# Retention and two expert layers on one core: moved refills, gathers, weight splits and row turns around the expert stage

## The chip, the cores and the metric

The kernel runs on one core of one Trainium2 chip. The metric is the device time of that core in microseconds (us), the median of several executions. TensorE (PE) multiplies matrices, its weight loads are shown apart as PEld, VectorE is DVE, ScalarE is ACT, GpSimd is POOL, and SyncE (SP) issues most of the plain transfers. POOL issues the gathers and scatters that go by a list of row numbers.

## The reference

```python
# stage 1: retention, per head a decayed state (q, k, v: 2 x 8 x 768 x 64)
state = gamma * state + k[t] v[t]^T ;  y[t] = scale * q[t] state
x = y as 1536 tokens x 512
# stage 2: a dense layer, 512 -> 2048 -> 512
h = x @ w_in ;  g = maximum(0.01 * h, h) ;  x = g @ w_out
# stage 3: 8 experts, each token goes to one of them; an expert takes at most capacity = 384 tokens
logits = x @ w_gate ;  e = argmax(logits) ;  gate = softmax(logits)[e]
for each expert: h = maximum(rows @ w1[e], 0) ;  y = h @ w2[e]        # 512 -> 1024 -> 512
out[token] = gate * y                                                # zero for tokens over capacity
```

## The kernel before, in words

All of it is one program, whose order on each engine is the order in which the code is written. The matrices are multiplied in split form: a value is a high part `hi` (made by ACT) and a low part `lo` (made by DVE), and three products are summed.

The dense layer works on units of 128 of the 2048 hidden columns for blocks of 384 tokens (`unit_h`, `unit_y`; lines 363 and 414 are its matmuls). Behind a block's last unit its rows go to `x2d` in HBM (`store_rows`), and `route` finds the expert of each token: logits, the one-hot `oh` (line 495), positions by a matmul (line 505).

Once three quarters of the tokens are routed, one expert is chosen ahead (`choose`). Its weights are gathered by POOL into `praw` (`pre_load`, line 668, eight gathers of 512 KB). `pre_split(k)` makes `hi` and `lo` of the second half of gather k (lines 345 and 346), and `pre_h`, `pre_y` compute one tile of 128 of its tokens while the last block is routed. Its rows come by a gather with the row numbers `pix` (line 649). `pre_end` finishes this, evacuates into `og` and scatters it (line 720).

Then come the experts in the order s = 0 to 7 (`expert`). An expert has eight weight units of 512 KB; unit u holds a slice of w1 and of w2. By the number of its tokens it has one, two or three tiles of 128 rows, and a body is written for each of these classes (`cls`); which one runs is decided on the chip by compare-and-branch, in the order two tiles, three tiles, one tile. In the profiled run the classes of s = 0 to 7 are 2, 3, 1, 1, 1, 1, 2, 2.

In a body, `mm_h` multiplies unit by unit (line 824, or line 818 for one tile, which takes the raw weights), `ew_h` makes `gh` and `gl` of its result, and `mm_y` (line 876) follows `LAGS[cls]` units later; a one-tile body does all eight `mm_h` first. `conv` splits the weight units to come (lines 846 and 847), up to three of the next expert among them. At step `PREP[cls]` the rows of the next expert are turned on PE (`prep_x`, line 772), copied by ACT and DVE (`cxh`, `cxl`, or `cxf` for one tile), and POOL gathers the rows of the expert after that (`load_x`, line 757). Each of these is itself a branch over the three classes (`by_class`, lines 745 and 748) on its engine.

The weights lie in 15 buffers (`land`, `xland`), filled in turn by SP. `refill` (line 884) loads the unit 15 further on into a buffer that `conv` has done with. In the first expert, `refills` returns until step `HOLD`, and the first refill waits for the last matmul of unit `HOLD`.

At step `NAME[cls]`, PE, ACT and DVE are given a hint of where the next expert's branch goes (`name_next`); it tells one tile from several, not two from three.

Of the kernel before, what the change touches and what calls it, by code (L numbers as in the profile page):

```python
# [59 lines left out]
def retention_moe_moe_kernel(ctx: ExitStack, tc: tile.TileContext, qkv, wb, wc, wg, const, out, cap):  # L60
    nc = tc.nc
    B, NCH = qkv.shape[0], qkv.shape[1]
    NF = wb.shape[0]
    E, PF = wc.shape[0], wc.shape[1]
# [11 lines left out]
    NS = E * slabs  # L76
# [253 lines left out]
    def conv_wc(u):  # L330
        craw[u] = landed["u", u]
        if NF + u not in wr:
            ring_tiles(NF + u)
        split(*wr[NF + u], craw[u])
# [381 lines left out]
    def pre_end():  # L716
        for k in (PF - 2, PF - 1):
            pre_y(k)
        nc.scalar.activation(out=pre_t["o"], in_=yps[0], func=ACTF.Copy, scale=pgate[:, 1, :])
        i = nc.gpsimd.indirect_dma_start(  # L720
            out=out, out_offset=bass.IndirectOffsetOnAxis(ap=pix, axis=0), in_=pre_t["o"], in_offset=None,
            bounds_check=NTOK - 1, oob_is_err=False)
        unordered("out", i)
# [3 lines left out]
    def fill_pe(n):  # L727
        for _ in range(n):
            pre_work.pop(0)()
# [23 lines left out]
    def load_x(s):  # L753
        xr = xr0[0]

        def gather(t):
            return nc.gpsimd.indirect_dma_start(
                out=xr[:, t, :], out_offset=None, in_=x2d,
                in_offset=bass.IndirectOffsetOnAxis(ap=gix[:, s * BT + t:s * BT + t + 1], axis=0),
                bounds_check=NTOK - 1, oob_is_err=False)  # L760

        if not regs:
            return [gather(t) for t in range(BT)][-1]
        by_class(s, 3, lambda c: [gather(t) for t in range(c)])
# [82 lines left out]
        nc.vector.tensor_tensor(out=lo[:, o], in0=src[:, o], in1=hi[:, o].bitcast(F32), op=ALU.subtract)  # L847

    LAGS = {1: PF, 2: 4, 3: 2}
    PREP = {1: 8, 2: 5, 3: 4}  # L850
    NAME = {1: 4, 2: 9, 3: 8}
    every = []

# [23 lines left out]
                                 start=(k == 0 and n == 0), stop=(k == PF - 1 and n == 2))  # L877

    held = [None]
    HOLD = 5  # L880

    def refill(u):
        if u < NU:
# [6 lines left out]
    def expert(s, cls, o):  # L890
        u0 = s * PF
        lag = LAGS[cls]
        last = s + 1 == NS
        todo = [(u, cls) for u in range(u0 + (1 if s == 0 else 3), u0 + PF)]
        todo += [(u, 2) for u in range(u0 + PF, min(NU, u0 + PF + 3))]
        filled = [u0]

        read = [u0]

        def conv_next():  # L900
            if todo and todo[0][0] < read[0] + RING + XRING:
                conv(*todo.pop(0))

        def hidden(k):
            u = u0 + k
            r = mm_h(u, cls)
            if u == HOLD:
                held[0] = r
            yield
            ew_h(u, cls)  # L910
            conv_next()

        def refills(k):
            if s == 0 and k < HOLD:
                return
            top = todo[0][0] if todo else u0 + PF
            while filled[0] < min(top, u0 + k + 1, u0 + PF):
                refill(filled[0] + LAND + XLAND)
                filled[0] += 1

        if s == 0:
            finish_all(prep_x(0, cls))
            pre_end()
            conv_next()
            conv_next()
            if NS > 1:
                load_x(1)
        xg = None
        for i in range(lag + PF):
            if i == NAME[cls] and not last:  # L930
                name_next(s + 1)
            if i == PREP[cls] and not last:
                xg = prep_x(s + 1)
                step(xg)
                if s + 2 < NS:
                    load_x(s + 2)
            h = hidden(i) if i < PF else None
            if h:
                step(h)
            k = i - lag  # L940
            if k >= 0 and not (last and k >= PF - 2):
                mm_y(u0 + k, cls, range(cls))
                read[0] = u0 + k + 1
            if h:
                step(h)
            else:
                conv_next()
            if i == PREP[cls] and xg is not None:
                finish_all(xg)
            refills(i)  # L950
        while todo:
            conv_next()
        refills(PF)
        for t in range(cls):
            if last:
                for v in (u0 + PF - 2, u0 + PF - 1):
                    mm_y(v, cls, [t])
            evac(s, o, t)
            scatter(s, o, t)
# [54 lines left out]
    with tc.manual_schedule():  # L1014
# [27 lines left out]
        def finish_all(g):  # L1042
            while step(g):
                pass
# [70 lines left out]
        for i in range(reached, len(units)):  # L1115
            ti, f = units[i]
            g, blk = tasks[ti]
            ensure(f, 0)
            unit_h(units[i])
            if ends(units[i]) and blk == PRE:  # L1120
                assert len(wdone) == 2 * NF
                mid.close()
                xr_p = ctx.enter_context(tc.tile_pool(name="xr", bufs=1))
                xr0.append(xr_p.tile([P, BT, DM], F32, name="xr"))
                nc.gpsimd.memset(xr0[0], 0.0)

            def slot():
                if g == NG - 1:
                    pre_load(2 * (blk + (units[i][1] == groups[g][-1])))
                    if len(praw) > 3 and len(psplit) < 2 * (i - first_pre - 4):  # L1130
                        pre_split(len(psplit))
                        pre_split(len(psplit))
                side_step()
                soon = [x for x in units[i + 1:i + 4] if (x[1], 0) not in wdone]
                pump(2 if soon else 1)

            slot()
            if i == len(units) - 1:
                break
            u = units[i - LAG]  # L1140
            ensure(u[1], 1)
            for t in range(BT):
                unit_y(u, t)
                if ends(u):
                    store_rows(tasks[u[0]][1], t)
                if t == 0:
                    slot()
            if ends(u):
                side.append(route(tasks[u[0]][1]))
            if i >= 24 and zr:  # L1150
                z = zr.pop(0)
                nc.sync.dma_start(out=z, in_=zero)
            slot()
        f1, f2, f3 = units[-3:]
        for u in (f1, f2, f3):
# [2 lines left out]
        pre_load(PF)  # L1158
        for n, (u, t) in enumerate(((f1, 0), (f2, 0), (f1, 1), (f2, 1), (f3, 0), (f1, 2), (f3, 1))):
            unit_y(u, t)  # L1160
            if n in (0, 1, 3, 5) and len(psplit) < 6:
                pre_split(len(psplit))
            side_step()
        while side:
# [28 lines left out]
        while side:  # L1193
            side_step()
        load_counts()
        for k in (6, 7):
            fill_pe(2)
            pre_split(k)
        conv_wc(0)
        fill_pe(len(pre_work))  # L1200
        ring_tiles(NF + 1)
        for b in yps[1:]:
            nc.tensor.matmul(out=b, lhsT=zb[:, 0:P], rhs=zb[:, 0:b.shape[1]], start=True, stop=True)
        for u in range(2, RING):
# [4 lines left out]
        xring_p.append(ctx.enter_context(tc.tile_pool(name="xring", bufs=XRING)))  # L1209

        pre_t["o"] = c_p.tile([P, DM], F32, tag="og", name="og", bufs=4)
        for u in range(1, LAND):
            craw[u] = landed["u", u]
        for u in range(RING, RING + XRING):
            ring_tiles(NF + u, xring_p[0])
# [85 lines left out]
```

## Time and profile before

| | |
|---|---|
| median of three runs | 546.14 us (546.31, 544.1, 546.14) |
| profiled execution | 544.94 us, of which the span shown is 543.1 us |
| PE busy | 514.3 us, 95% of the span |
| mean granted clock of TensorE | 0.982 of full speed |
| bytes moved by DMA | 80.77 MB, 149 GB/s over the span |

Times in the views are from the start of the span. The retention and the dense layer run to about 331 us, the routing and the expert chosen ahead to about 358 us, and the eight experts to the end. A wait in brackets behind a row is idle time of that engine just before it, with what ended it; "issue" stands for time in which the engine waited for nothing that the profile shows.

### The profile page before, as it was taken

How to read it: one execution, taken by the hardware profiler on the slowest of the kernel's cores; microseconds unless marked ns; L12 is line 12 of the kernel's file. 1: busy time of each engine (PE TensorE's matmuls, PEld its weight loads, DVE VectorE, ACT ScalarE, POOL GpSimd, SP SyncE). 2: the span in 40 equal slices, each digit the busy share in tenths (PEclk: the TensorE clock that was granted, in tenths of full speed). 3: DMA queues.
4: the chain of work that ended last, by engine and by line, in shares of the span. 5: the costliest groups of instructions: out<-in, count | busy, mean ns of one | idle time of the engine just before them, and what ended most of it. 6: DMA issues, size and time to landing. Idle time of an engine off the chain costs nothing.

```text
span 543.1 us, 8948 instructions
## 1 busy us (share of the span) xinstructions
PE 514.3 (95%) x3316; PEld 462.6 (85%) x3318; DVE 339.1 (62%) x670; ACT 240.6 (44%) x501; POOL 50.4 (9%) x75
## 2 busy tenths in 40 slices
PE   8899999999999999999999998999399989999995
PEld 6888989998999899989999997988299978889893
DVE  4999993379689559947444257477044456566560
ACT  2877963354344334423231324285043445555450
POOL 0000000000000000000001063331100211120101
PEclk9999999999999999999999998999789999989999
DMA  8986781022234502401111056666633288992001
GB/s 318 371 279 235 236 268 41 1 79 87 88 114 138 194 1 81 150 4 42 37 58 60 1 187 239 197 221 226 247 110 97 88 340 318 328 309 85 11 22 42
DMA packets 24938, 80.77 MB, mean 149 GB/s; under 512 B 3706, under 2 KB 3834, under 8 KB 24864
## 3 DMA queue, kind: packets, MB, share of 16 engines
q1 hardware_dynamic: 21312, 70.26, 37.4%
q0 software_dynamic: 3552, 9.58, 4.9%
q8 instruction: 39, 0.64, 0.5%
q14 instruction: 35, 0.29, 0.2%
HBM read 72.35 MB, written 9.96 MB: 152 GB/s over the span
## 4 chain that ended last, share of the span: by engine, by line
PE 72%; DMA 22%; issue 2%; DVE 2%; ACT 1%; SPq 0%; POOL 0%; ACTq 0%; POOLq 0%; DVEq 0%
PE ps_h L363 25%; PE ps_y L414 18%; DMA out<-og,gix 12%; DMA xr<-x2d,gix 7%; PE ps_a L414 7%; PE ps_y L876 5%; PE ps_h L824 5%; PE ps_a L256 2%; PE ps_a L190 2%; PE ps_a L463 1%; PE ps_a L245 1%; PE ps_h L702 1%; DMA early<-qkv 1%; PE ps_y L713 1%; DMA land<-qkv 1%
## 5 line engine op out<-in xcount | busy, mean ns | idle before, releaser
L370 ACT ACTIVATE hs<-ps_h 128x384 f32<-128x384 f32 x64 | 31.4, 491 | 111.5 <-PE ps_h L363 111.5
L375 DVE SCALAR_TENSOR_TENSOR hs<-hs 128x384 f32<-128x384 f32 x64 | 35.6, 556 | 70.5 <-ACT hs L370 70.2
L414 PE MATMUL ps_y<-hi,gh 128*128 128x512 f32 x138 | 57.0, 413 | 0.0
L363 PE MATMUL ps_h<-xh,hi 128*128 128x384 f32 x256 | 55.8, 340 | 0.0
L414 PE MATMUL ps_y<-lo,gh 128*128 128x512 f32 x138 | 55.1, 399 | 0.0
L414 PE MATMUL ps_y<-hi,gl 128*128 128x512 f32 x138 | 55.0, 399 | 0.0
L363 PE MATMUL ps_h<-xh,lo 128*128 128x384 f32 x256 | 54.9, 337 | 0.0
L363 PE MATMUL ps_h<-xl,hi 128*128 128x384 f32 x256 | 54.8, 336 | 0.0
L379 ACT ACTIVATE gh<-hs 128x384 fp32r<-128x384 f32 x64 | 33.7, 526 | 43.1 <-DVE hs L375 43.1
L363 PEld LDWEIGHTS ps_h<-xh,hi 128*128 128x128 f32 x256 | 45.9, 188 | 5.3
L385 DVE TENSOR_TENSOR gl<-hs,gh 128x384 fp32r<-128x384 f32 x64 | 35.6, 556 | 21.3 <-ACT gh L379 21.3
L363 PEld LDWEIGHTS ps_h<-xl,hi 128*128 128x128 f32 x256 | 45.4, 188 | 0.0
L363 PEld LDWEIGHTS ps_h<-xh,lo 128*128 128x128 f32 x256 | 45.3, 188 | 0.0
L847 DVE TENSOR_TENSOR lo<-xland,hi 128x1024 fp32r<-128x1024 f32 (+1 forms) x32 | 33.6, 1054 | 12.8 <-ACT hi L846 12.2
L876 PE MATMUL ps_y<-hi,gh 128*128 128x512 f32 x104 | 41.2, 396 | 0.0
L876 PE MATMUL ps_y<-hi,gl 128*128 128x512 f32 x104 | 41.0, 394 | 0.0
L876 PE MATMUL ps_y<-lo,gh 128*128 128x512 f32 x104 | 40.8, 393 | 0.0
L847 DVE TENSOR_TENSOR lo<-land,hi 128x1024 fp32r<-128x1024 f32 (+1 forms) x31 | 32.4, 1048 | 12.5 <-ACT hi L846 12.4
L867 DVE SCALAR_TENSOR_TENSOR gl<-ps_h,gh 128x256 fp32r<-128x256 f32 (+2 forms) x42 | 16.5, 394 | 32.7 <-ACT gh L866 32.5
L866 ACT ACTIVATE gh<-ps_h 128x256 fp32r<-128x256 f32 (+2 forms) x42 | 15.2, 363 | 44.1 <-PE ps_h L824 29.4
L846 ACT ACTIVATE hi<-land 128x1024 fp32r<-128x1024 f32 (+1 forms) x31 | 28.3, 915 | 7.9 <-issue 3.0
L846 ACT ACTIVATE hi<-xland 128x1024 fp32r<-128x1024 f32 (+1 forms) x32 | 29.3, 921 | 5.4 <-PE ps_y L876 5.4
(198 smaller groups left out, 997.4 us busy)
## 6 DMA issues: line engine op xcount, KB each, us to landing
land<-wc SPq DMA_DIRECT2D x32, 512.0 KB, 5.6
xland<-wc SPq DMA_DIRECT2D x32, 512.0 KB, 5.0
land<-wb SPq DMA_DIRECT2D x31, 512.0 KB, 5.0
land<-qkv SPq DMA_DIRECT2D x19, 512.0 KB, 5.6
out<-zero SPq DMA_DIRECT2D x12, 256.0 KB, 6.2
x2d<-rows SPq DMA_DIRECT2D x12, 256.0 KB, 2.1
early<-qkv SPq DMA_DIRECT2D x5, 512.0 KB, 7.2
cst<-cst_in SPq DMA_DIRECT2D x1, 512.0 KB, 5.5
```

The source lines that it names most:

```text
L363: nc.tensor.matmul(out=h_ps, lhsT=w[i][:, dc * P:(dc + 1) * P], rhs=x[j][:, dc, :], start=(n == 0), stop=(n == 3 * KD - 1))
L370: nc.scalar.activation(out=hs, in_=gt[u][0], func=ACTF.Copy)
L375: nc.vector.scalar_tensor_tensor(out=hs, in0=hs, scalar=0.01, in1=hs, op0=ALU.mult, op1=ALU.max)
L379: nc.scalar.activation(out=gh, in_=gt[u][0], func=ACTF.Copy)
L385: nc.vector.tensor_tensor(out=gl, in0=hs, in1=gh.bitcast(F32), op=ALU.subtract)
L414: nc.tensor.matmul(out=yb[ti][t], lhsT=gt[u][i][:, t * P:(t + 1) * P], rhs=w[j][:, 512:1024], start=(f == fs[0] and n == 0), stop=(f == fs ...
L824: r = nc.tensor.matmul(out=hp, lhsT=w[i][:, dc * P:(dc + 1) * P], rhs=(h, l)[j][:, dc, 0:cls * P], start=(n == 0), stop=(n == 3 * KD - 1))
L846: nc.scalar.activation(out=hi[:, o], in_=src[:, o], func=ACTF.Copy)
L847: nc.vector.tensor_tensor(out=lo[:, o], in0=src[:, o], in1=hi[:, o].bitcast(F32), op=ALU.subtract)
L866: nc.scalar.activation(out=gh, in_=hp, func=ACTF.Relu)
L867: nc.vector.scalar_tensor_tensor(out=gl, in0=hp, scalar=0.0, in1=gh.bitcast(F32), op0=ALU.max, op1=ALU.subtract)
L876: nc.tensor.matmul(out=yps[t], lhsT=gg[i][:, t * P:(t + 1) * P], rhs=w[j][:, 512:1024], start=(k == 0 and n == 0), stop=(k == PF - 1 and n ...
```

## The change

Five things are changed. `HOLD` goes from 5 to 1, so that the first refills wait for the second unit's matmuls of the first expert. The gathers of the second expert's rows (`load_x(1)`) are issued ahead of `pre_end`, whose scatter is on the same queue. The first three `pre_split` stand ahead of the dense layer's last `slot` and no longer behind its last unit, and the other three of the six at other steps of the tail. The last two are put between single steps of the chosen expert, and unit 1 is split there too, together with unit 0, and no longer in the first expert's body. `PREP` of one-tile bodies goes from 8 to 6.

```diff
-    PREP = {1: 8, 2: 5, 3: 4}
+    PREP = {1: 6, 2: 5, 3: 4}
-    HOLD = 5
+    HOLD = 1
-        todo = [(u, cls) for u in range(u0 + (1 if s == 0 else 3), u0 + PF)]
+        todo = [(u, cls) for u in range(u0 + (2 if s == 0 else 3), u0 + PF)]
         if s == 0:
             finish_all(prep_x(0, cls))
+            if NS > 1:
+                load_x(1)
             pre_end()
             conv_next()
-            conv_next()
-            if NS > 1:
-                load_x(1)
                     pre_load(2 * (blk + (units[i][1] == groups[g][-1])))
-                    if len(praw) > 3 and len(psplit) < 2 * (i - first_pre - 4):
-                        pre_split(len(psplit))
-                        pre_split(len(psplit))
+            if i == len(units) - 2:
+                for k in range(3):
+                    pre_split(k)
             slot()
-            if n in (0, 1, 3, 5) and len(psplit) < 6:
+            if n in (2, 3, 5):
                 pre_split(len(psplit))
-        for k in (6, 7):
-            fill_pe(2)
-            pre_split(k)
-        conv_wc(0)
+        fill_pe(1)
+        pre_split(6)
+        fill_pe(1)
+        pre_split(7)
+        for u in range(2):
+            fill_pe(1)
+            conv_wc(u)
         fill_pe(len(pre_work))
-        ring_tiles(NF + 1)
-        for u in range(1, LAND):
+        for u in range(2, LAND):
             craw[u] = landed["u", u]
```

On DVE, in the tail of the dense layer, this piece of the difference runs from the last but one unit (its `gl` stands just ahead) to the one-hot of the last but one block. `lo<-xpre` is a `pre_split`, `pix` the row numbers for the gather of the chosen expert's rows, `hs` and `gl` belong to the last unit, and `mx` begins the way to `oh`. Before:

```order
L645 TENSOR_TENSOR p_3418<-tab,ahead 128x16
L646 TENSOR_REDUCE pgate<-p_3418 128x2
L647 TENSOR_SCALAR none<-pgate 128x1
L648 SCALAR_TENSOR_TENSOR pix<-pgate,none 128x1
L375 SCALAR_TENSOR_TENSOR hs<-hs 128x384
L385 TENSOR_TENSOR gl<-hs,gh 128x384
L346 TENSOR_TENSOR lo<-xpre,hi 128x512 x2
L657 TENSOR_TENSOR d_3465<-tab 128x16x2
```

The same place in the changed kernel:

```order
L346 TENSOR_TENSOR lo<-xpre,hi 128x512 x3
L645 TENSOR_TENSOR p_3428<-tab,ahead 128x16
L646 TENSOR_REDUCE pgate<-p_3428 128x2
L647 TENSOR_SCALAR none<-pgate 128x1
L648 SCALAR_TENSOR_TENSOR pix<-pgate,none 128x1
L375 SCALAR_TENSOR_TENSOR hs<-hs 128x384
L385 TENSOR_TENSOR gl<-hs,gh 128x384
L657 TENSOR_TENSOR d_3469<-tab 128x16x2
```

The three splits moved ahead of `pix` and of the last unit; ACT's `hi<-xpre` moved ahead of its `hs` and `gh` of that unit in the same way.

On ACT, a one-tile body from its last units to the copy of the next expert's rows; `gh` is a unit's result, `hi<-xland 128x1024` a split for the next expert, the rows with `cxh` and `cxf` are the branch over the next expert's class. Before:

```order
L866 ACTIVATE gh<-ps_h 128x128
L866 ACTIVATE gh<-ps_y 128x128
L745 UNCONDITIONAL_BRANCH
L866 ACTIVATE gh<-ps_y 128x128
L846 ACTIVATE hi<-xland 128x1024
L745 UNCONDITIONAL_BRANCH
L745 COMPARE_AND_BRANCH
L775 ACTIVATE cxh<-ps_a 128x4x128 x3
L745 UNCONDITIONAL_BRANCH
L748 COMPARE_AND_BRANCH
L775 ACTIVATE cxh<-ps_a 128x4x128 x2
L748 UNCONDITIONAL_BRANCH
```

The same place in the changed kernel:

```order
L745 UNCONDITIONAL_BRANCH
L866 ACTIVATE gh<-ps_h 128x128
L745 UNCONDITIONAL_BRANCH
L866 ACTIVATE gh<-ps_y 128x128
L745 COMPARE_AND_BRANCH
L775 ACTIVATE cxh<-ps_a 128x4x128 x3
L745 UNCONDITIONAL_BRANCH
L748 COMPARE_AND_BRANCH
L775 ACTIVATE cxh<-ps_a 128x4x128 x2
L748 UNCONDITIONAL_BRANCH
```

The branch moved ahead of the last unit's `gh` and of the first split for the next expert; both now stand behind it, with the two other splits.

## Rows read from the trace of the kernel before

**Rows 1.** The page, part 1: busy time, share of the span and instructions of each engine.
```profile
PE 514.3 (95%) x3316; PEld 462.6 (85%) x3318; DVE 339.1 (62%) x670; ACT 240.6 (44%) x501; POOL 50.4 (9%) x75
```

**Rows 2.** Waits of PE, 318 to 543 us: total, times, longest.
```profile
PE ps_h L824 <- issue: 9.1, 1, 9.1
PE ps_y L818 <- DVE lo L847: 3.3, 3, 1.9
PE ps_a L505 <- DVE oh L495: 2.1, 1, 2.1
PE ps_h L818 <- DVE cxf L790: 1.5, 1, 1.5
PE ps_h L824 <- DVE lo L847: 0.5, 1, 0.5
PE ps_h L824 <- ACT hi L846: 0.3, 1, 0.3
```

**Rows 3.** Timeline of PE, second unit of s = 0 and start of s = 1.
```profile
362.37 0.63 PE L824 MATMUL ps_h<-cxl,hi 128*128 128x256 f32 x4
...
392.98 1.62 PE L824 MATMUL ps_h<-cxh,hi 128*128 128x384 f32 x4 [9.10 <-issue]
...
396.96 1.16 PE L824 MATMUL ps_h<-cxh,hi 128*128 128x384 f32 x4
...
398.65 0.86 PE L824 MATMUL ps_h<-cxl,hi 128*128 128x384 f32 x4
```

**Rows 4.** Windows of 2 us; last three columns: granted clock, DMA share, GB/s.
```profile
382.00:384.00 2.00, 1.89 (x9) 1.17 (x7) 0.07 (x1) 0.69 (x1) 0.00 (x0) 1.00 1.03 410
...
388.00:390.00 2.00, 0.00 (x0) 0.00 (x0) 0.00 (x0) 0.00 (x0) 0.00 (x0) 0.50 0.60 205
```

**Rows 5.** Timeline of SP's queue, 371 to 385 us: the first refills.
```profile
371.41 3.43 SPq L884 DMA_DIRECT2D land<-wc  x7
374.93 10.14 SPq L884 DMA_DIRECT2D xland<-wc  x4
```

**Rows 6.** DMA issues at 374.9 us: size, us from issue to landing.
```profile
xland<-wc SPq DMA_DIRECT2D x1, 512.0 KB, 10.5
```

**Rows 7.** DMA queues, 388.5 to 389.5 us: packets, MB, share.
```profile
q8 instruction: 2, 0.03, 20.8%
```

**Rows 8.** Timeline of ACT at the end of the first three one-tile bodies.
```profile
437.54 1.06 ACT L846 ACTIVATE hi<-xland 128x1024 fp32r<-128x1024 f32 x1 [0.86 <-PE ps_y L876]
442.62 0.38 ACT L783 ACTIVATE cxf<-ps_a 128x256 f32<-128x256 f32 x1 [4.02 <-issue]
...
453.19 1.06 ACT L846 ACTIVATE hi<-land 128x1024 fp32r<-128x1024 f32 x1 [0.86 <-PE ps_y L876]
...
458.27 1.06 ACT L846 ACTIVATE hi<-land 128x1024 fp32r<-128x1024 f32 x1 [2.80 <-PE ps_h L818]
...
467.44 1.06 ACT L846 ACTIVATE hi<-xland 128x1024 fp32r<-128x1024 f32 x1 [0.85 <-PE ps_y L876]
...
472.41 1.06 ACT L846 ACTIVATE hi<-xland 128x1024 fp32r<-128x1024 f32 x1 [3.65 <-PE ps_y L876]
```

**Rows 9.** Timeline of PE where the fourth one-tile body begins.
```profile
472.05 1.95 PE L818 MATMUL ps_h<-cxf,xland 128*128 128x128 f32 x16
475.91 3.62 PE L818 MATMUL ps_y<-cxf,xland 128*128 128x128 f32 x16 [1.92 <-DVE lo L847]
```

**Rows 10.** DMA issues at 318.70 us, the third gather of weights: us to landing.
```profile
xpre<-wc,wix POOLq DMA_INDIRECT x1, 7.7
```

**Rows 11.** Timelines of ACT and of DVE in the dense layer's tail.
```profile
325.78 0.49 ACT L370 ACTIVATE hs<-ps_h 128x384 f32<-128x384 f32 x1 [3.28 <-PE ps_h L363]
...
321.75 0.17 DVE L646 TENSOR_REDUCE pgate<-p 128x2 f32<-128x16 f32 x1
...
327.97 1.29 DVE L346 TENSOR_TENSOR lo<-xpre,hi 128x512 fp32r<-128x512 f32 x2
...
330.50 0.17 DVE L488 TENSOR_REDUCE mx<-ps_a 128x3 f32<-128x24 f32 x1
```

## The prediction

> **What bounds the kernel now.** I read the page first: PE is busy for 514.3 of 543.1 us [rows 1]. It is the bound nearly throughout, so a change can give back only PE's idle time and the stretches in which its clock is low. The list of PE's waits from the tail of the dense layer on [rows 2] shows where these are, and the reader should see how few they are: one of 9.1 us, one of 2.1, and six that sum to 5.6 (3.3 + 1.5 + 0.5 + 0.3). Then I read the timeline around each, to see what ended it and how fast PE was behind it [rows 3, 9], the windows and transfers beside the longest one [rows 4 to 7], ACT at the ends of one-tile bodies [rows 8], and the tail [rows 10, 11].
>
> The profiled execution took 544.94 us, 1.2 below the median of the runs (546.14), so the sum below is made against 544.94, and the median may come out up to 1.2 higher than its result.
>
> **HOLD from 5 to 1.** The longest wait stands where s = 1, a three-tile expert, begins: PE goes on at 392.98 after 9.10 us with nothing to wait for but "issue" [rows 3]. Two packets of an instruction queue fall into 388.5 to 389.5 [rows 7], so I read the gap as program code being loaded: the hint ahead of the branch does not tell two tiles from three, and the three-tile body lies behind another one. The gap began at 383.9; some 4.6 us passed until the packets, and 4 more until PE went on. In the first part the DMA engines were full, 1.03 at 382 to 384 and still 0.60 at 388 to 390 [rows 4]. What filled them are the first refills: seven from 371.41 and four from 374.93 [rows 5], one of which took 10.5 us to land [rows 6].
>
> With HOLD = 1 the first refill no longer waits for unit 5 but for unit 1, whose matmuls ended at 363.0 [rows 3], so the eight refills of s = 0 begin 8 us earlier or a little more. At the 410 GB/s of a full window [rows 4] their 4.2 MB need 10 us, and they are done near 374. The refills of s = 1 that SP issues ahead follow one at a time. At PE's jump the transfers are then nearly idle. I take the first part of the gap from 4.6 to 1.5 us (an estimate between nothing and 4.6, nearer to nothing because a code packet has little to move) and leave the second: a gain of **3.1**. The clock is another matter. The first matmuls of s = 1 took 1.62 us per four, at half clock [rows 4], against 0.86 later [rows 3]; the twelve up to 396.96 took 3.98 where 2.1 would do. A gap of 6 us leaves that 1.9 us loss in place, since a wait of 1.92 brought it too (below). The bounds are 0, and 9.1 + 1.9 = 11.0 if the gap vanishes.
>
> On this the Trainium skill has a rule that speaks against the gain. The page "Runtime: NRT & Kernel Launch", section "Instruction fetch mechanics", says that an engine fetches its code through a DMA queue of its own, and that a taken branch out of the loaded window must wait for a fetch. The trace agrees with the wait, by the 9.1 us [rows 3]. If a queue of its own means that refills don't delay it, this term is 0.
>
> The cost of the earlier refills is that they lie beside the gathers of the second expert's rows. These are now issued ahead of `pre_end` and of its scatter on POOL's queue, so they start some us earlier as well. The turn that needs them stands just ahead of unit 5, near 368. I cost it at nothing; the cover is the five units of PE work before. Without it, a gather issued near 361 that took 10.5 like a refill [rows 6] would be 3.5 late. The scatter itself is now some 4 us later, and nothing reads it before the end.
>
> **Unit 1 split earlier.** PE's waits of 0.5 and 0.3 [rows 2] are the second unit of s = 0 waiting for its `lo` and `hi`. These are now made beside the last matmuls of the chosen expert, where ACT and DVE have room: **0.8**, with 0 as the other end, if the split (1.06 us on ACT for a unit, [rows 8]) is late there.
>
> **Three splits sooner.** Before, ACT's `hs` of the last unit starts at 325.78 and DVE's `mx` at 330.50 [rows 11], 4.7 later; in between stand three `lo` of about 0.65 each (1.29 for two). PE waits 2.1 us for what follows from `mx` [rows 2]. Now the splits stand ahead of `hs`, but the third gather lands only at 318.70 + 7.7 = 326.4 [rows 10]. ACT's third `hi` (half a unit, so 0.6 by the 1.06 of a whole one, [rows 8]) then runs to 327.0 and `hs` begins 1.2 later than before. DVE ends the third `lo` near 327.7, has four small operations to `pix` (0.17 each and a gap, 0.8 together, [rows 11]) and reaches the last unit's `hs` at 328.5, 1.0 later than it could. From there the way to `mx` is 2.0 shorter. In sum 1.2 + 1.0 - 2.0 = 0.2, and I take a **loss of 0.3**; bounds -1 (the gather lands sooner) and +1. The gather of the chosen expert's rows leaves 3 us later, but stands behind the weight gathers in its queue anyway.
>
> **PREP from 8 to 6.** In each one-tile body ACT stands still for a while behind the branch over the next class. Its first split for the next expert starts at 437.54, 453.19 and 467.44, and ACT goes on 5.1, 5.1 and 5.0 us later [rows 8], the first time with "issue" as the reason, at the copy `cxf`; the other times it got one or two operations further. I read this as code being loaded too, 5 us behind the branch each time. PE pays where the next body begins: 1.5 for `cxf`, and 3.3 in three waits for DVE's `lo` [rows 2]. The longest, 1.92, also lowered the clock: 16 matmuls took 3.62 instead of 1.95 [rows 9], 1.7 more. The whole is 6.5 us.
>
> With PREP = 6 the branch runs behind the seventh unit's `gh`: earlier by one `mm_h` (0.9, half of 1.95, [rows 9]) and one `mm_y` (0.7: seven of them lie between ACT's split at 467.44, [rows 8], and the next body at 472.05, [rows 9]), 1.6 in all. Where ACT's stop lies behind `cxf` (the second and third time), the splits end 1.6 sooner, and the waits of 0.9 and 1.9 shrink to 0 and 0.3, the clock stays up: 0.9 + 1.6 + 1.7 = **4.2**. The first time the stop is at `cxf`. If it stays there, `gh` of the last unit and three splits come behind it instead of two; `cxf` is in time, but the last `lo` is only 0.3 sooner, and PE, that no longer waits 1.5 at the start, waits some 2 us two units on. If code of the same place in memory is what is late, the stop moves behind `gh` and the 2.0 are won. I take 0 for it, between +2 and -1.7 (the clock). The cover on PE is the eight `mm_y`, 5.3 us: they don't need what stands behind the stop, except the last, which needs the last `gh`.
>
> **The sum.** 3.1 + 0.8 - 0.3 + 4.2 = 7.8, so 544.94 - 7.8 = 537.1, and I forecast **537**.
>
> **The rivals.**
> - The code fetch of s = 1 doesn't depend on refills: 537 + 3.1 = **540**. For it speaks that packets did move at 388.5 while the engines were still 0.60 busy; against it, that half of the gap had passed before the first of them. This is where the skill's rule above leads.
> - The gap at s = 1 shrinks to nothing: 537 - 7.9 = **529**. Against it speaks the 4 us from the packets to the first matmul, with DMA no longer full.
> - The gathers of s = 1 come late beside the refills: 537 + 3.5 = **540.5**, with the wait on the turn in s = 0.
> - Neither stop changes, since each takes its time wherever the branch stands: only 0.8 - 0.3 remain, **544.4**.
> - Slower: ACT's stop lies at the copy in all four one-tile bodies. Then three splits come behind it each time, and PE waits 2 us plus 1.7 of clock at four starts, 14.8 instead of 6.5. That is 8.3 lost, against 3.1 + 0.8 - 0.3 won: **549.6**. It decides from the point at which the stop begins ahead of `cxf` in three of the four. In the trace it did so once in the three shown [rows 8].
>
> **How the numbers follow.** The forecast has a chance of 0.45 (its own range is 534 to 539.5), the independent fetch 0.22, late gathers 0.08, the vanished gap 0.08, no change in either stop 0.10, slower 0.07. Of 544.94 or of the median, 0.5% is 2.7 us, about what a measurement of this kernel can tell. Faster by more than that: 0.45 + 0.22 + 0.08 + 0.08, less 0.03 for mixtures, 0.80. Slower: 0.07. The rest, 0.13, within. The range leaves out the slower case and half of the vanished gap and of no change: 531 to 543.5.
>
> **What would show it.** In the changed profile the refills from line 884 should begin near 362, and DMA be light around PE's start of s = 1; the wait on "issue" there should be 5 to 7 us, with a low clock behind it. The waits of line 818 for `cxf` should be gone, those for `lo` be under 2 in total, and the slow matmuls at the fourth one-tile body gone. The waits of line 824 in s = 0 should be gone, and that of line 505 stand at 2 to 2.7. Wrong would make it: a gap at s = 1 that is still 9 us with idle DMA, a new wait of line 772 on a gather, or `cxf` that still comes last.

## Result and the profile after

The changed kernel takes 537.5 us (median of 4 runs, 536.41 to 537.65) against 545.12 us (4 runs, 543.17 to 546.31): a ratio of 0.9859, with a 95% interval of 0.9823 to 0.9896. The profiled execution took 537.65 us with a span of 535.9, 7.2 less than the span before, 543.1.

The page of the changed kernel, part 1, beside [rows 1]:

```profile
PE 513.2 (96%) x3318; PEld 461.9 (86%) x3318; DVE 338.4 (63%) x670; ACT 240.3 (45%) x501; POOL 50.7 (9%) x75
```

PE works nearly as long as before; what went is idle time. Waits of PE from the tail of the dense layer on, in the changed kernel (total, times, longest), which answer to [rows 2]:

```profile
PE ps_h L824 <- issue: 6.4, 1, 6.4
PE ps_a L505 <- DVE oh L495: 2.5, 1, 2.5
PE ps_y L818 <- DVE lo L847: 1.8, 3, 1.1
PE ps_a L463 <- DVE xt L697: 0.4, 1, 0.4
PE ps_h L818 <- DVE lo L847: 0.2, 1, 0.2
```

The wait on issue is 2.7 shorter, those of line 818 fall from 4.8 to 2.0, those of line 824 on `hi` and `lo` are gone. The wait of line 505 is 0.4 longer, and one of 0.4 at line 463 is new.

SP's queue in the changed kernel, the first refills; compare [rows 5]:

```profile
363.63 5.89 SPq L884 DMA_DIRECT2D land<-wc  x7
371.30 14.03 SPq L884 DMA_DIRECT2D xland<-wc  x4
```

They begin 7.8 us earlier. Windows of 2 us around PE's jump into s = 1 (last columns: granted clock, DMA share, GB/s), against [rows 4]:

```profile
378.00:380.00 2.00, 2.00 (x10) 1.67 (x9) 1.57 (x3) 1.33 (x2) 0.00 (x0) 1.00 0.00 0
...
382.00:384.00 2.00, 2.00 (x10) 1.39 (x8) 0.00 (x0) 0.51 (x1) 0.00 (x0) 1.00 0.77 219
...
388.00:390.00 2.00, 0.00 (x0) 0.00 (x0) 0.00 (x0) 0.00 (x0) 0.00 (x0) 0.66 0.59 224
...
392.00:394.00 2.00, 2.00 (x8) 2.00 (x7) 0.00 (x0) 0.00 (x0) 0.00 (x0) 0.50 0.00 0
```

The eight refills of s = 0 are over by 378 (the prediction had 374). But those of s = 1 and the scatters of s = 0 are on the engines at the jump, so DMA is not idle there, 0.77 where it was 1.03. The clock is still half of full behind the wait. PE there, to be read beside [rows 3]:

```profile
383.75 0.40 PE L876 MATMUL ps_y<-hi,gl 128*128 128x512 f32 x1
390.56 1.62 PE L824 MATMUL ps_h<-cxh,hi 128*128 128x384 f32 x4 [6.41 <-issue]
...
395.66 0.86 PE L824 MATMUL ps_h<-cxh,lo 128*128 128x384 f32 x4
```

ACT at the ends of the first two one-tile bodies, the counterpart of [rows 8]:

```profile
434.49 0.38 ACT L783 ACTIVATE cxf<-ps_a 128x256 f32<-128x256 f32 x1 [0.56 <-issue]
434.77 0.27 ACT L866 ACTIVATE gh<-ps_y 128x128 fp32r<-128x128 f32 x1
438.78 2.95 ACT L846 ACTIVATE hi<-xland 128x1024 fp32r<-128x1024 f32 x3 [3.74 <-PE ps_y L876]
...
449.37 0.39 ACT L783 ACTIVATE cxf<-ps_a 128x256 f32<-128x256 f32 x1 [0.46 <-issue]
...
453.45 2.01 ACT L846 ACTIVATE hi<-land 128x1024 fp32r<-128x1024 f32 x2 [2.17 <-PE ps_y L876]
```

The stop is still there, and it is not for PE that ACT waits, although the list puts it down to line 876: the wait ends 1.5 us behind the start of a packet of another instruction queue, q14 (changed kernel, 437.3 to 437.4 us; queue, packets, MB, share):

```profile
q14 instruction: 1, 0.01, 19.3%
```

I take q14 for ACT's queue, because this holds for every such stop: 49 of more than 2 us lie at the ends of one-tile bodies in the profiles listed below, and each ends 1.35 to 1.84 us behind the start of a packet of q14. In the changed kernel the copy (`cxf`, in the fourth body `cxh`) and the last `gh` now stand ahead of the stop, in all four bodies. And the start of the fourth, with the slow matmuls of [rows 9], runs at full clock:

```profile
468.38 1.95 PE L818 MATMUL ps_h<-cxf,xland 128*128 128x128 f32 x16
470.82 2.05 PE L818 MATMUL ps_y<-cxf,xland 128*128 128x128 f32 x16 [0.49 <-DVE lo L847]
```

From such starts the span splits into stages. All numbers are us, from one profiled execution of each kernel: where the first matmul of s = 0 starts, how long s = 0 then takes PE, its wait on issue at s = 1, the sum of its waits of line 818 on `lo`, `gl` and `cxf`, and the stretch from the first matmul of s = 2 to the end of the span. Ratios are to the kernel before, run on the same occasion; its own median went from 544.66 to 546.21 between occasions, so medians of different rows compare less well than their ratios.

| kernel | s = 0 at | s = 0 takes | wait at s = 1 | line 818 | s = 2 to end | median | ratio (95%) |
|---|---|---|---|---|---|---|---|
| before | 358.65 | 25.2 | 9.1 | 4.8 | 114.0 | 545.12 | 1 |
| changed | 359.83 | 24.3 | 6.4 | 2.0 | 109.1 | 537.5 | 0.9859 (0.9823 to 0.9896) |
| e1_hold5 | 358.17 | 24.4 | 9.4 | 2.8 | 109.8 | 540.18 | 0.9897 (0.9849 to 0.9945) |
| e2_prep8 | 358.58 | 24.4 | 4.8 | 6.3 | 116.9 | 543.81 | 0.9960 (0.9936 to 0.9984) |
| e3_tail | 360.87 | 24.4 | 5.9 | 2.7 | 109.5 | 538.41 | 0.9864 (0.9822 to 0.9906) |
| e4_quiet | 358.44 | 24.4 | 5.0 | 2.4 | 109.6 | 535.53 | 0.9814 (0.9760 to 0.9867) |
| e5_hint | 360.18 | 23.9 | 4.3 | 3.5 | 115.0 | 539.98 | 0.9885 (0.9848 to 0.9923) |
| e6_fall | 359.40 | 23.9 | 1.4 | 2.4 | 110.3 | 532.32 | 0.9757 (0.9709 to 0.9805) |
| e7_prep5 | 361.35 | 23.9 | 6.5 | 1.6 | 108.1 | 536.88 | 0.9826 (0.9787 to 0.9866) |
| e9_one_first | 357.58 | 23.9 | 5.7 | 5.6 | 114.0 | 540.11 | 0.9899 (0.9838 to 0.9960) |
| e10_unit1 | 358.16 | 25.3 | 6.3 | 4.5 | 112.9 | 541.86 | 0.9927 (0.9896 to 0.9958) |
| e11_fall_prep5 | 359.81 | 23.9 | 1.1 | 1.0 | 110.3 | 533.82 | 0.9773 (0.9713 to 0.9833) |
| e12_same | 359.30 | 23.9 | 7.0 | 2.2 | 109.3 | 537.68 | 0.9857 (0.9794 to 0.9920) |
| e13_shift | 358.13 | 24.0 | 6.5 | 0.4 | 105.8 | 532.70 | 0.9790 (0.9761 to 0.9819) |

For the change this gives +1.2 up to s = 0, -0.9 in s = 0, -2.7 at s = 1, +0.1 in its body (36.1 to 36.2), -4.9 from s = 2 on: -7.2.

### The profile page after: what moved, and what is told of

Read it like the earlier page. It is cut to its first block, busy times and chain, and to the rows that moved or that the text cites. A ratio compares the mean times of both kernels' runs of the same rounds, so it can differ in the third digit from the quotient of the medians.

```text
span 535.9 us, 8952 instructions
## 1 busy us (share of the span) xinstructions
PE 513.2 (96%) x3318; PEld 461.9 (86%) x3318; DVE 338.4 (63%) x670; ACT 240.3 (45%) x501; POOL 50.7 (9%) x75
## 4 chain that ended last, share of the span: by engine, by line
PE 70%; DMA 18%; issue 5%; DVE 4%; ACT 1%; POOL 1%; POOLq 0%; another core or an unknown queue 0%; ACTq 0%; DVEq 0%
PE ps_h L363 24%; PE ps_y L414 16%; DMA out<-og,gix 8%; DMA xr<-x2d,gix 7%; PE ps_a L414 7%; PE ps_y L876 5%; PE ps_h L824 5%; PE ps_a L256 2%; PE ps_a L190 2%; PE ps_h L702 2%; DMA xpre<-wc,wix 1%; PE ps_a L463 1%; PE ps_a L245 1%; PE ps_y L713 1%; PE ps_y L1021 1%
## 5 line engine op out<-in xcount | busy, mean ns | idle before, releaser
L370 ACT ACTIVATE hs<-ps_h 128x384 f32<-128x384 f32 x64 | 31.4, 491 | 108.1 <-PE ps_h L363 108.1
L847 DVE TENSOR_TENSOR lo<-xland,hi 128x1024 fp32r<-128x1024 f32 (+1 forms) x32 | 33.5, 1054 | 13.1 <-ACT hi L846 12.0
L847 DVE TENSOR_TENSOR lo<-land,hi 128x1024 fp32r<-128x1024 f32 (+1 forms) x30 | 31.1, 1043 | 10.0 <-ACT hi L846 8.5
L414 PEld LDWEIGHTS ps_y<-hi,gl 128*128 128x128 f32 x138 | 25.9, 188 | 5.8
```

The costliest lines, as they stand in the source:

```text
L370: nc.scalar.activation(out=hs, in_=gt[u][0], func=ACTF.Copy)
L414: nc.tensor.matmul(out=yb[ti][t], lhsT=gt[u][i][:, t * P:(t + 1) * P], rhs=w[j][:, 512:1024], start=(f == fs[0] and n == 0), stop=(f == fs ...
```

## The experiments

My theory: the wait at s = 1 and ACT's stops are code that arrives late; the first is longer when refills fill the DMA engines, the second cost PE less when the branch runs sooner. The rivals: the fetch doesn't depend on refills, and the stops go with the branch or the load.

**HOLD alone back (e1_hold5).**

```diff
-    HOLD = 1
+    HOLD = 5
```

> The changed kernel with HOLD back at 5, nothing else. Theory (the code that PE lacks at s = 1 comes slowly when refills fill the DMA engines): PE's wait on issue at the start of s = 1 goes from 6.4 back to about 9 us, with the DMA engines near full from 376 to 386, and the time rises by 2.7 us, from 537.5 to 540.2. Rival (the code fetch does not depend on refills; the 2.7 us came from the other edits, which moved the jump by a fraction of a microsecond): the wait stays at 6.4 and the time at 537.5.

The theory held for the wait: 9.36 us. The median rose by 2.7, but the intervals of the two ratios overlap, so it is the wait that decides.

```profile
382.15 0.40 PE L876 MATMUL ps_y<-hi,gl 128*128 128x512 f32 x1
391.91 1.62 PE L824 MATMUL ps_h<-cxh,hi 128*128 128x384 f32 x4 [9.36 <-issue]
```

**No refill at the jump (e4_quiet).**

```diff
-            if s == 0 and k < HOLD:
+            if (s == 0 and k < HOLD) or (s == 1 and k < 1):
...
-            if u == HOLD:
+            if u in (HOLD, PF):
```

> The changed kernel with the first refill of s = 1 held until the first matmul of s = 1 has run, so that no refill is on the DMA engines when PE jumps into the three-tile body; only the scatters of s = 0 and code are. Theory (what is left of the wait still holds a part that refills cause: the DMA engines were 0.72 to 0.77 busy at 380 to 384): the wait on issue falls from 6.4 to about 4.5 to 5, the time by 1.5 to 2. Rival (6.4 is what a jump into code that is not there costs by itself): the wait stays at 6.4 within 0.3 and the time within 0.5 of 537.5.

The wait was 4.96. Where it is made shows in the packets of an instruction queue, q8, which I take for PE's because they fit PE's waits. With refills held off, both packets began to move within 0.6 us of the end of s = 0 at 382.82 (queue, packets, MB, share; 383.2 to 383.6):

```profile
q8 instruction: 2, 0.03, 66.4%
```

Read from each kernel's trace: from the end of s = 0 to the start of the first packet behind it, and from there to PE's next matmul.

| kernel | from the end to the packet | from the packet to PE |
|---|---|---|
| before, e1_hold5 (HOLD = 5) | 4.9, 5.1 | 4.2, 4.2 |
| changed, e3, e7, e9, e10, e12, e13 | 1.4 to 1.9 | 4.2 to 5.4 |
| e2_prep8, e4_quiet | 0.3, 0.5 | 4.5, 4.5 |

The first part is long where refills fill the DMA engines (HOLD = 5). Between the other two rows the load does not decide: in the microsecond behind the end of s = 0 the engines were 0.33 busy in e2_prep8, but also only 0.39 and 0.40 in e9 and e7. What differs is the packet ahead of this one. It began 3.2 and 3.3 us before the end in e2 and e4, 1.5 to 1.7 before it in the second row, and the next followed 3.1 to 3.8 us behind it in all nine. Why it came sooner in e2, whose edit has nothing to do with this place, is open.

The second part is no fixed price either. Two packets move in each of the eleven, and PE's next matmul starts 1.6 to 2.2 us behind the end of the later one. The part is longest, 4.9 to 5.4, in the four kernels whose second packet came 2.2 to 2.7 us behind the first.

Executions with HOLD = 1 differ, 4.8 to 7.0 in eight of them, mean 6.1, against 9.1 and 9.4. So one wait of 4.96 does not show that the refills left at the jump still cost something (e2_prep8, with them there, waited 4.76), nor does the median, 2.0 lower with an interval that overlaps the changed kernel's.

**A second hint (e5_hint).** In `name_next`, for s = 1 (and a label `two1` on the second branch):

```diff
             tc.mark_branch_hint_location(f"many{s}", hint=over(s, e, 1), engines=[e])
+            if s == 1:
+                tc.mark_branch_hint_location("two1", hint=regs[ENGS.index(e)][s // slabs] <= (s % slabs) * BW + 2 * P, engines=[e])
```

> The changed kernel with a second hint on PE, ACT and DVE behind the first one in s = 0: it names the branch between two and three tiles of s = 1, which until now had none. Theory (PE's wait at s = 1 is made of the time until a request for code is answered, 0.3 to 5 us by what else moves, and some 4.4 us from the first packet on, and all of it passes behind the jump because nothing asks for the three-tile body sooner): the wait falls from 4.8 to 6.4 to under 1 us, the half-clock stretch behind it goes too, and the time falls by 6 to 8 us, to 530. Rival (a second hint isn't used, or what is late is more than the code at the jump's target): the wait stays at 4.8 to 6.4 and the time within 1.5 of 537.5.

The theory fell, at least for this hint: 4.29 us are left. One packet still moved behind the jump, where the kernels above had two, and PE went on 2.7 us behind its start. And the time rose by 2.5, for another reason. ACT, in three one-tile bodies (two shown):

```profile
436.99 0.38 ACT L783 ACTIVATE cxf<-ps_a 128x256 f32<-128x256 f32 x1 [5.27 <-issue]
```

```profile
452.00 0.39 ACT L783 ACTIVATE cxf<-ps_a 128x256 f32<-128x256 f32 x1 [4.45 <-issue]
```

The stop is at the copy again, with PREP at 6. The hint had made ACT's program 6 instructions longer; that this moved the stop is argued, since ACT also executes the hint.

**Falling into three tiles (e6_fall).** For s = 1 alone the bodies are written in the other order:

```diff
+                first, second = (3, 2) if s == 1 else (2, 3)
-                with tc.If(n <= base + 2 * P, preferred_fallthrough_block=True) as two:
-                    expert(s, 2, o)
+                with tc.If(n > base + 2 * P if s == 1 else n <= base + 2 * P, preferred_fallthrough_block=True) as two:
+                    expert(s, first, o)
                 with two.Else():
-                    expert(s, 3, o)
+                    expert(s, second, o)
```

> The changed kernel with the two bodies of s = 1 in the other order: the three-tile body directly behind the first branch, so that this input falls into it and no jump over the two-tile body is taken. Theory (the jump to code that nobody asked for is the cause): the wait on issue at s = 1 is under 1 us and the time falls by 6 to 8 us, to 530. Rival (three-tile code is missing whichever way it is reached, since PE runs no code like it before): a wait of 4 us or more stays, and the time within 2 of 537.5.

The jump was the cause, though the gain fell short of the theory (1.40 instead of under 1, and 5.2 of the 6 to 8 us in the median). PE goes on at full clock, 0.86 us per four:

```profile
384.74 0.93 PE L824 MATMUL ps_h<-cxh,hi 128*128 128x384 f32 x4 [1.40 <-issue]
385.51 0.86 PE L824 MATMUL ps_h<-cxh,lo 128*128 128x384 f32 x4
```

A packet of q8 began 1.8 us behind the end of s = 0 here too (385.05 to 385.15), when PE was already at work. So the first packet in the table above need not be one that the jump asks for:

```profile
q8 instruction: 1, 0.02, 60.8%
```

Part of the wait comes back at the end of the body, from which a longer jump now leads over two others to s = 2 (2.6 in e11_fall_prep5, which has the same order):

```profile
PE ps_h L818 <- issue: 2.2, 1, 2.2
```

The order suits the three tiles of this input; s = 0 and the last two experts have two.

**PREP (e2_prep8, e7_prep5).**

```diff
-    PREP = {1: 6, 2: 5, 3: 4}
+    PREP = {1: 8, 2: 5, 3: 4}    # e2_prep8; 5 in e7_prep5
```

> The changed kernel with PREP of one-tile bodies back at 8. Theory (ACT's stop behind the branch is worth 4.4 us in the four one-tile bodies and 0.4 in the sixth): the waits of line 818 come back to about 4.8 in total, the copy cxf among them, the slow matmuls behind the longest too, and the time rises by 4.4 to 4.8, to 542.1. Rival (the stop goes where DMA load puts it, and the earlier refills alone have moved it): the waits stay near 2.0 and the time rises by under 1.

The waits of line 818 came back and more, 6.3 where the kernel before had 4.8, and the stretch from s = 2 took 7.8 longer, not 4.8. The row of ACT in the first one-tile body:

```profile
437.28 0.38 ACT L783 ACTIVATE cxf<-ps_a 128x256 f32<-128x256 f32 x1 [4.49 <-issue]
```

> The changed kernel with PREP of one-tile bodies at 5 instead of 6. Theory (ACT's stop begins a fixed piece of code behind that branch, so that an earlier branch brings the splits behind it forward by another 1.6 us): the waits of line 818 fall from 2.0 to 2.6 in total to under 0.6, and the time by 1.5 to 3, to 535. Rival (the stop now lies on the last gh, which the last matmuls of the body need, and PE waits for these instead): new waits of line 876 for gh appear, 1 to 2 us in each of four bodies, and the time rises by 2 or more.

1.0 less from s = 2 on, and no new wait of line 876. Line 818 still waits 1.6, where the theory had under 0.6, and the median can't be told from PREP = 6.

**The small branch (e9_one_first).**

```diff
-        with tc.If(rv > base + 2 * P) as c1:
-            fn(3)
+        with tc.If(rv <= base + P, preferred_fallthrough_block=True) as c1:
+            fn(1)
         with c1.Else():
-            with tc.If(rv > base + P) as c2:
-                fn(2)
+            with tc.If(rv > base + 2 * P) as c2:
+                fn(3)
             with c2.Else():
-                fn(1)
+                fn(2)
```

> The changed kernel with the cases of the small branches ahead of a turn (line 745, in by_class) in another order: one tile comes first, so that a one-tile expert falls into its case and jumps over the two others behind it, where before it jumped twice to reach its case. Theory (ACT's stop of 3.5 to 4.5 us in one-tile bodies is code that the two jumps of this branch have to bring): the stops shrink to under 1 us where the next expert has one tile, the waits of line 818 (2.0 in total) go, and the time falls by 1.5 to 3, to 535. Rival (the stop is code of the one-tile body itself, reached in order, a piece that is loaded too late whatever the branch does): the stops stay at 3.5 to 4.5 us and the time within 1 of 537.5.

The theory fell. `cxf` no longer waits 0.5, but the stops stay, and three of the four are longer; with 540.11 us the rival's time was missed too. ACT, first one-tile body:

```profile
430.97 0.38 ACT L783 ACTIVATE cxf<-ps_a 128x256 f32<-128x256 f32 x1
...
436.81 2.95 ACT L846 ACTIVATE hi<-xland 128x1024 fp32r<-128x1024 f32 x3 [4.88 <-PE ps_y L876]
```

So the jumps of that branch are not what ACT waits for. ACT's last tasks of the body end no sooner, and PE loses 4.9 from s = 2 on.

**Unit 1 alone back (e10_unit1).**

```diff
-        todo = [(u, cls) for u in range(u0 + (2 if s == 0 else 3), u0 + PF)]
+        todo = [(u, cls) for u in range(u0 + (1 if s == 0 else 3), u0 + PF)]
...
             pre_end()
             conv_next()
+            conv_next()
...
-        for u in range(2):
-            fill_pe(1)
-            conv_wc(u)
+        fill_pe(2)
+        conv_wc(0)
```

> The changed kernel with unit 1 of s = 0 split behind pre_end again, as before the change; the second expert's gathers stay ahead of it. Theory (unit 1's split in s = 0 is late for PE by 0.8 us, and the two splits at once delay what follows a little more): the waits of line 824 on hi and lo come back with 0.8 us, the body of s = 0 takes 25.2 instead of 24.3 to 24.4 us, and the time rises by 0.9. Rival (the earlier gathers or the earlier refills shortened that body): no wait comes back and the body stays at 24.4.

In s = 0 as expected, 25.3 us with waits of 1.0 and 0.3; the twelve profiles with the early split have 23.9 to 24.4. But the stretch from s = 2, which the edit doesn't touch, took 3.8 longer. ACT, first one-tile body:

```profile
433.13 0.38 ACT L783 ACTIVATE cxf<-ps_a 128x256 f32<-128x256 f32 x1 [0.56 <-issue]
437.29 0.28 ACT L866 ACTIVATE gh<-ps_y 128x128 fp32r<-128x128 f32 x1 [3.78 <-PE ps_y L876]
```

The stop is one operation sooner, ahead of the last `gh`, which the last matmuls of the body need. ACT's program behind s = 0 is 2 instructions longer here. I then counted in each kernel the number, in the order of ACT's program (from 0, instructions that only wait for or set a semaphore left out), of the instruction with which it goes on behind each stop:

```text
kernel           length of program   s = 2      s = 3     s = 4     s = 5
before                 1151          574 cxf    682 hi    786 hi    892 hi
changed                1149          573 hi     680 hi    785 hi    891 hi
e2_prep8               1149          572 cxf    679 hi    784 hi    890 hi
e5_hint                1155          576 cxf    681 cxf   786 cxf   893 gh
e9_one_first           1149          573 hi     680 hi    785 hi    891 hi
e10_unit1              1151          574 gh     680 hi    785 hi    892 hi
```

The operations differ, the numbers hardly: 572 to 576, 679 to 682, 784 to 786, 890 to 893, in these and in the other kernels so far, whatever PREP and the branch do. But the programs differ by 6 instructions at most, and each of these bodies ends within some 6 of the same number too. So the numbers alone don't tell a place in the program from the end of a body; the next run was to.

**ACT's code moved, nothing executed changed (e13_shift).**

```diff
+        if s == 0 and cls == 1:
+            dead = sm_p.tile([P, 1], F32, name="dead", bufs=1)
+            for _ in range(22):
+                nc.scalar.activation(out=dead, in_=bias_e, func=ACTF.Copy)
         if s == 0:
             finish_all(prep_x(0, cls))
```

> The changed kernel with 22 tiny ACT instructions in the one-tile body of s = 0, which this input never runs: nothing that is executed differs, but all of ACT's code behind that body lies 22 instructions later. Theory (ACT's stops lie at fixed numbers of its program, near 573, 680, 785 and 891 in every kernel so far, because code of that place comes late): the stops hit the operations that stood 22 earlier, in the first half of the one-tile bodies (a gh of the fourth or fifth unit), where PE has several units ahead of it; the copies and splits at the ends of the bodies are in time, the waits of line 818 fall from 2.0 to 2.2 to under 0.8, and the stretch from the start of s = 2 to the end falls from 109.1 to 109.8 to 106.5 to 108. Rival (the stop belongs to the branch over the next class or to the operations behind it, wherever they lie): the stops stay behind that branch and the stretch stays at 109.1 to 109.8.

The gain was larger than expected: 105.8 from s = 2 on, 3.4 less than the changed kernel, and 532.7 in the median, 5 less. Of the 5.7 between the two spans, 1.7 lie ahead of s = 0, within the spread of the tail shown below. ACT, first one-tile body:

```profile
427.80 0.28 ACT L866 ACTIVATE gh<-ps_h 128x128 fp32r<-128x128 f32 x1 [2.49 <-PE ps_y L818]
...
432.85 0.38 ACT L783 ACTIVATE cxf<-ps_a 128x256 f32<-128x256 f32 x1 [0.47 <-issue]
433.13 0.27 ACT L866 ACTIVATE gh<-ps_y 128x128 fp32r<-128x128 f32 x1
433.69 2.96 ACT L846 ACTIVATE hi<-xland 128x1024 fp32r<-128x1024 f32 x3 [0.30 <-PE ps_y L876]
```

No stop stands behind `cxf`. Some 2 us are lost at the first `gh`, behind the jump into the body, and PE waits 0.4 for it, in a body that takes 13.9 where the changed kernel takes 13.1; in the next two bodies ACT's longest idle time in front of a `gh`, copy or split is 1.05. The part of the theory by which the stops would only move 22 operations up is wrong: they went. The packets of q14 show what happened: the last one of this body began at 431.75, 1.1 us ahead of `cxf`, where in the changed kernel it began at 437.31, 2.8 us behind `cxf`. In the next three bodies no packet begins between the copy and the last split. So the code of the bodies' ends was there in time. All that PE still waits for behind the tail's 2.4 is this:

```profile
PE ps_h L824 <- issue: 6.5, 1, 6.5
...
PE ps_h L818 <- DVE gl L867: 0.4, 1, 0.4
```

**The tail alone back (e3_tail), and the changed kernel again (e12_same).** The six `pre_split` in the order of before, unit 1 still early:

```diff
+                    if len(praw) > 3 and len(psplit) < 2 * (i - first_pre - 4):
+                        pre_split(len(psplit))
+                        pre_split(len(psplit))
...
-            if i == len(units) - 2:
-                for k in range(3):
-                    pre_split(k)
...
-            if n in (2, 3, 5):
+            if n in (0, 1, 3, 5) and len(psplit) < 6:
```

> The changed kernel with the six splits of the tail in the order of before; unit 1 of s = 0 is still split early. Theory (the moved splits cost time, 0.4 at the wait of line 505 and the rest by a stretch at half clock that falls onto longer work): line 505 waits 2.1, the first matmul of s = 0 starts at 358.65 instead of 359.83, and the time falls by 1.2 to 536.3. Rival (the splits must be early for unit 1 to be in time, and the half-clock stretch comes anyway): the first matmul of s = 0 starts at 359.5 or later, or waits of line 824 come back in s = 0, and the time stays within 0.4 of 537.5.

> The changed kernel as it is, once more, to see how far one execution of it differs from the next. Theory (what differs is where the half-clock stretch of the tail falls, and how far the refills and scatters lie in the way of the code at s = 1): the first matmul of s = 0 starts anywhere from 358.2 to 361.4, the wait on issue at s = 1 is 4.8 to 6.5, and the body of s = 0 takes 24.3 to 24.4 and the stretch from s = 2 to the end 109.1 to 109.7 as before. Rival (the stages keep their times, and the differences seen so far came from the edits): the first matmul of s = 0 starts at 359.8 and the wait is 6.4, each within 0.2.

Line 505 waits 2.1 with the old order, but s = 0 starts later than in the changed kernel, at 360.87, and the median is 0.9 higher, not 1.2 lower. The same tail code started it anywhere from 357.58 to 361.35 in eleven executions (median 359.30), the old order at 358.65 and 360.87. A stretch at half clock falls into the tail each time, at one of two places: at 330 to 338 in eight of the fourteen profiles, where s = 0 then starts at 357.58 to 359.30, and at 340 to 348 in six, where it starts at 359.40 to 361.35. What decides between them is open. In the changed kernel's profile it lies here (granted clock third from the end):

```profile
340.00:342.00 2.00, 2.00 (x15) 1.96 (x14) 0.75 (x2) 0.00 (x0) 0.00 (x0) 0.71 0.02 7
342.00:344.00 2.00, 2.00 (x12) 2.00 (x11) 0.42 (x1) 0.45 (x2) 0.00 (x0) 0.50 0.33 124
```

In the kernel before it lay at 332 to 336, just behind the wait of line 505. The +1.2 of this pair of profiles lies within that spread. The second execution of the changed kernel had the stretch at 332 to 336, so the same program can have either; it waited 6.96 at s = 1, over the 6.5 of the expectation, and took 109.3 from s = 2 on.

**Both together (e11_fall_prep5).** The edits of e6_fall and e7_prep5.

> The changed kernel with both edits that gave time so far: the three-tile body of s = 1 first, so that it is fallen into, and PREP of one-tile bodies at 5. Theory (the two act in different stages and add): s = 1 starts within 2 us of the end of s = 0 at full clock, the stretch from s = 2 to the end is 1 us shorter than with PREP at 6, and the time is 531. Rival (the other order of the bodies moves ACT's code, and its stops fall onto the copy again, so that PREP = 5 gains nothing or loses): cxf waits on issue for 4 us or more in a one-tile body, and the time is 532.5 or more.

They don't add: 110.3 from s = 2 on as in e6_fall, and a median that can't be told from it. The rival's reason doesn't hold either: no `cxf` is late. What the second body gains (14.1 against 15.6 in e6_fall) the first loses, 14.8 against 13.2: behind the wait of 2.6 at its start the granted clock was 0.71 and 0.50 of full at 422 to 426, where in e6_fall, behind 2.2, it stayed at 1.00. The last split of the fourth body is late in both, by stops of 4.53 and 4.40. The three-tile order with the shifted code was not tried.

## Why the prediction was right, step by step

- **HOLD.** 3.1 was forecast, 2.7 came in the two profiles, 3.1 as the difference of the means (9.2 and 6.1). The split of the gap was right: a part until the first packet that refills lengthen (4.9 and 5.1, then 1.4 in the mean of eight, forecast 1.5) and one of 4 to 5 behind it. What filled the engines at the jump afterwards, refills of s = 1 and scatters, was not in it, so "nearly idle" was wrong (0.77 busy); the half clock behind the gap stayed, as forecast. The rival of an independent fetch is out by e1_hold5.
- On this the Trainium skill ("Runtime: NRT & Kernel Launch", "Instruction fetch mechanics") has each engine fetch through a queue of its own. The trace shows such queues, and also that the first packet came some 3.6 us later behind the end of s = 0 when refills filled the DMA engines (means of 5.0 in the two profiles with HOLD = 5 and 1.4 in the eight above with HOLD = 1).
- **Unit 1.** 0.8 forecast, 0.9 in the two profiles, 1.0 with e10_unit1. That the place of the split also moves ACT's later code was not seen; e10_unit1 took 3.8 more from s = 2 on.
- **Three splits sooner.** A loss of 0.3 forecast; ACT's third `hi` did wait for the gather, until 326.63. The effect can't be told from the spread of the tail.
- **PREP.** 4.2 forecast, 4.9 from s = 2 on. The third and fourth one-tile bodies, where the 4.2 was to come from (0.9 and 3.3), are 0.7 and 3.1 shorter, the latter with the clock that stayed up. The first was put at 0 and is 1.7 shorter (14.8 to 13.1): there the stop moved behind `gh`, as the sentence on code of the same place had it. The second is 1.0 longer, by a new wait of 1.1 for `lo`, and the remaining 0.4 lies at the start of s = 6. The reason was only half right: "I read this as code being loaded too, 5 us behind the branch each time". Code it is, but not tied to the branch: e13_shift leaves the branch and moves the code, and the stops go.
- Luck has a part. The same PREP with 6 more instructions on ACT (e5_hint) took 115.0 from s = 2 on, more than the kernel before (114.0), and with 22 more (e13_shift) 105.8; nothing in the prediction chose between these. And a hit within 0.5 us is finer than the spreads of the tail (357.58 to 361.35) and of the wait at s = 1 (4.8 to 7.0), so to that degree it is chance.
- The slower rival, the stop at the copy in every body, is not far off: e5_hint had it in three.
- The gathers of s = 1: no wait of line 772 appeared.

What stays open: why 22 more instructions bring ACT's packets sooner, what decides when a packet is asked for, and why the hint does not take the wait at s = 1 away. That code is what arrives late for ACT rests on the packets of q14 behind which all 49 stops end, and on e13_shift, where packets and stops went together.

## What to carry to other kernels

A wait on "issue" behind a taken branch is looked up in the packets of the engine's instruction queue. Here moving other transfers away from the jump brought the packets sooner (9.2 to 6.1 us of waiting on average), and falling through instead of jumping took away most of the rest (1.4 and 1.1 us left). With long unrolled bodies for several cases, an edit anywhere ahead moves the code of all bodies behind it, and here the single edits undone don't add up ( 2.7, 6.3, 4.4 and 0.9 by the medians, in sum 14.3, or 11.6 by the ratios, where the whole change gave 7.6); compare them by stages, and try a few instructions that are never run before crediting a reordering. And a single profile of a stage with a half-clock stretch can be off by some us: repeat it before pricing an edit in it.

## What the hardware showed unexpectedly

- Code that is never executed, 22 instructions of it on one engine, changed the median by 5 us of 537.5 (0.9859 to 0.9790 of before); 3.4 of it lie in the stretch from s = 2 on, where ACT's stops went.
- ACT stopped for up to 5.3 us near the ends of one-tile bodies, at nearly the same numbers of its program in every kernel but e13_shift, and each time until 1.35 to 1.84 us behind the start of a packet of its instruction queue. The Trainium skill (same page and section) calls the crossing from one block of code to the next mostly hidden; if these stops are such crossings, which no run here shows, the trace disagrees.
- From the first code packet to PE's next matmul 4.2 to 5.4 us passed, also with the DMA engines only 0.28 busy over the wait (4.5 in e4_quiet); from the end of the second packet it was 1.6 to 2.2 us.
